# Attention values placed behind the next pair's scores, and their block sums multiplied in 64x32 tiles

## The chip, the core and the metric

The kernel runs on one core of a Trainium2 chip. The core has five engines that run side by side, each through its own instruction stream: TensorE (PE, matrix products out of SBUF into PSUM; its weight loads are shown apart as PEld), VectorE (DVE), ScalarE (ACT), GpSimd (POOL) and SyncE (SP, which here issues the transfers). [...] The metric is the device time of one execution in microseconds (us), lower is better.

## What is computed

Two blocks follow each other. The first is a sparse attention over 4 batches, 8 heads, 768 tokens and 64 numbers per head. Each token attends to the tokens less than 16 away, and to 24 sums, one for each block of 32 tokens (the maximum of the block's keys, the mean of its values):

```python
k_sum = k.reshape(B, H, nb, block, D).max(axis=3)
v_sum = v.reshape(B, H, nb, block, D).mean(axis=3)
scores_l = scale * (q @ k^T), outside |i - j| < 16 set to -1e9
scores_s = scale * (q @ k_sum^T) + log(block)
a = softmax over [scores_l, scores_s]
x = a @ concat([v, v_sum])
```

The second block takes x as (4, 768, 512), adds to it the real part of its two-dimensional Fourier transform (u), normalises each row, and applies two dense layers of 512 to 2048 to 512 with a ReLU between, added to u. All is in 32-bit floats.

## The kernel before

The dense layers are most of PE's work. For each batch they run in four phases: `gen_hidden(b, 0)`, `gen_out(b, 0)`, `gen_hidden(b, 1)`, `gen_out(b, 1)`, each over half of the 2048 inner columns. The products are of blocks two by two with seven multiplications; L1368 is the one of the hidden layer (128x128 weights, 384 columns), L1437 the one of the output layer (256 columns), L1414 batch 0's output. DVE and ACT add up the partial results from PSUM (L571, in the helper `tt`, and L1379 to L1398), and four PSUM buffers rotate among them, so a late DVE stops PE in the end.

Attention of batch b+1 is woven into the dense phases of batch b as a generator, `gen_attention`: `drive` advances both by so many steps (`yield`s), 80 of attention to 44 of the dense work for batches 2 and 3. Where in PE's stream the attention lands thus depends on the count of yields. Behind that a scheduler fixes the order of each engine's instructions when the program is built, by its own estimate of readiness; it can also cut a visit in pieces, with dense matmuls between them.

The heads go in four pairs (g = 0 to 3) for each batch. For one pair of batches 1 to 3 there are two visits to PE:

- *scores*: `scores` (L791, 48 matmuls in 64x64 tiles of the array: two heads, two halves of the tokens, blocks of 32 queries against 64 keys around them), then ACT's exponential of each half (L797) and DVE's multiplication by the mask `near` (L571); and `sum_scores` (L808, 4 matmuls in 64x32 tiles: queries against the block maxima) with its exponential (L809).
- *values*: `scale_sums` (L814: one matmul picks the pair's block sums of v into PSUM, and ACT writes them twice into `vs`, L816), then `values`: 48 matmuls in 64x32 tiles of 65 columns (L826, the probabilities of one block against its values and a column of ones), and 6 matmuls in 64x128 tiles of 130 columns (L831, the probabilities of the block sums against `vs`), into the same two PSUM tiles `av`. DVE takes the reciprocal of the sums (L836) and writes the scaled result into x (L571).

Every 32-bit matmul is two passes of the hardware, each with its weight load, so the profile's counts are twice those above. A tile of 64x32 uses a quarter of the array's columns and half of its rows: eight of them stand in the array at once.

The tag `attn` has four PSUM buffers, given out in the order of the code: `vs`, the two halves of the scores, the sum scores, the two `av`. The probabilities `p` have two buffers. Loads of values (`load_values`), of dense weights and of q and k stand in one queue on SP, in the order of issue. Batch 0 has another form (`wide_values`) that the change doesn't touch.

For batches 2 and 3 the last pair is followed by `turn_tiles`: two of x's token tiles go out to DRAM and come back with the tokens in mirrored order (L954 and L955, issued by POOL), and `fold_batch` then adds and subtracts halves of x for the Fourier transform, on DVE, with the returned tiles as `xr`. Between the two stand a number of yields.

Of the kernel before, what the change touches and what calls it, by code (L numbers as in the profile page):

```python
# [16 lines left out]
P = 128  # L17
# [471 lines left out]
def _main_program(ctx, tc, q, k, v, moe_w_ch1, moe_w_ch2, out):  # L489


    nc = tc.nc
# [6 lines left out]
    NP = H // 2  # L499
# [6 lines left out]
    HT = NST // 2  # L506
# [35 lines left out]
    vs = cpool.tile([P, 2, D1], FP, name="vs")  # L542
# [13 lines left out]
    def abank(shape, name):  # L556
        return psum.tile(shape, FP, tag="attn", bufs=4, name=name)
# [12 lines left out]
    def tt(out, in0, in1, op):  # L570
        return nc.vector.tensor_tensor(out=out, in0=in0, in1=in1, op=op).ins  # L571
# [28 lines left out]
    def room(name):  # L600
        return bpool.tile([P, NC * 2 * S], FP, tag="room", name=name)
# [62 lines left out]
    def load_values(b, g):  # L664
        if is_wide(b):
            load_wide_values(b, g)
            return
        load_narrow_values(b, g)

    def load_wide_values(b, g):  # L670

        vw, off = wide_vw(g), v[b, 2 * g].offset
        for r0, r1, i0, i1 in ((0, WK, 1, NQ - 1), (W, WK, 0, 1), (0, WK - W, NQ - 1, NQ)):
            for e in range(2):
                fetch(out=vw[r0:r1, e, i0:i1, 0:D],
                      in_=bass.AP(v.tensor, off + (S * e + QB * i0 - W + r0) * D,
                                  [[D, r1 - r0], [QB * D, i1 - i0], [1, D]]))

    def load_narrow_values(b, g):


        vw = vw_bufs[g % 2]
        if g < 2 and is_wide(b - 1):
            nc.gpsimd.memset(vw[:, :, D:D1], 1.0)
        for e in range(2):
            off = v[b, 2 * g + e].offset
            for h in range(2):
                r, i = 64 * (e ^ h), NB2 * h
                last = (b, g, e, h) == (B - 1, NP - 1, 1, 1)
                if last:  # L690

                    fetch(out=vw[r + 64 - W:r + 64, i:nb - 1, 0:D],
                                      in_=bass.AP(v.tensor, off + (BLOCK * i + 64 - 2 * W) * D,
                                                  [[D, W], [BLOCK * D, NB2 - 1], [1, D]]))
                n = 64 - W if last else 64
                fetch(out=vw[r:r + n, i:i + NB2, 0:D],
                                  in_=bass.AP(v.tensor, off + (BLOCK * i - W) * D, [[D, n], [BLOCK * D, NB2], [1, D]]))

    def key_maxima(g):
        nc.vector.tensor_reduce(out=km_bufs[g % 2][:, 0:nb], in_=kt_bufs[g % 2][:, W:W + S].rearrange("p (n f) -> p n f", f=BLOCK),  # L700
                                op=ALU.max, axis=AX.X)
# [100 lines left out]
    def sum_scores(b, g, p):  # L802
        km, qt = km_bufs[g % 2], nat[b, g]
        ps = abank([P, S2], f"ss_{b}_{g}")
        for h in range(2):
            for e in range(2):
                rows, r = slice(D * e, D * (e + 1)), 64 * (e ^ h) + 32 * h
                nc.tensor.matmul(ps[r:r + 32, :], km[rows, :], qt[rows, S2 * h:S2 * (h + 1)], start=True, stop=True)  # L808
        nc.scalar.activation(out=p, in_=ps, func=AF.Exp, scale=SC)  # L809

    def scale_sums(b, g):
        ps = abank([P, D], f"vs_{b}_{g}")
        vb, pick = sums[b, g]
        nc.tensor.matmul(ps, pick, vb, start=True, stop=True)  # L814
        for r in range(2):
            nc.scalar.activation(out=vs[:, r, 0:D], in_=ps, func=AF.Identity, scale=half_of[:, r:r + 1])  # L816

    def values(b, g, p, pm, x):
        vw = vw_bufs[g % 2]
        av = [abank([P, NST, D1], f"av_{b}_{g}_{r}") for r in range(2)]  # L820
        for t in range(NST):
            h = t // HT
            for j in range(4):
                for r in range(2):
                    rows, i = slice(64 * r, 64 * (r + 1)), 4 * t + j
                    nc.tensor.matmul(av[r][32 * j:32 * (j + 1), t, :], p[rows, h, i - NB2 * h, :], vw[rows, i, :],  # L826
                                     start=(t == 0), stop=False, skip_group_check=True)
        for t in range(HT):
            for r in range(2):
                rows = slice(64 * r, 64 * (r + 1))  # L830
                ins = nc.tensor.matmul(av[r][:, t:t + HT + 1:HT, :], pm[rows, P * t:P * (t + 1)], vs[rows],  # L831
                                       start=False, stop=(t == HT - 1), skip_group_check=True)
        marks["av", b, g] = ins.ins
        for r in range(2):
            rc = rec[:, b * NP + g, r]
            nc.vector.reciprocal(out=rc, in_=av[r][:, :, D])  # L836
            xo = x[:, 0, P * g + D * r:P * g + D * (r + 1)]
            xo = bass.AP(xo.tensor, xo.offset, [list(xo.ap[0]), [HT * DM + D * (1 - 2 * r), 2], [DM, HT], [1, D]])
            tt(xo, av[r].rearrange("p (h t) d -> p h t d", h=2)[:, :, :, 0:D],
               rc.rearrange("p (h t) -> p h t", h=2)[:, :, :, None].to_broadcast([P, 2, HT, D]), ALU.mult)  # L840
# [3 lines left out]
    def following(b, g, n):  # L844
        i = b * NP + g + n
        return divmod(i, NP) if i < B * NP else None
# [59 lines left out]
    def split_fold(b, fold):  # L906

        n = 3 * HT * DM
        zqs[b] = fold[:, n:n + 2 * HT * P].rearrange("p (r t m) -> p r t m", r=2, t=HT)
        return fold[:, 0:n].rearrange("p (i t d) -> p i t d", i=3, t=HT)  # L910
# [76 lines left out]
    def gen_attention(b):  # L987
        x = bpool.tile([P, NST, DM], FP, tag="x", bufs=2, name=f"x_{b}")
        x_of[b] = x
        held = None  # L990
        if b == 2:
            load(2, 1)
            load(2, 2)
        if b > 1:
            yield
            yield
            with tc.issue_after(marks["load"]):
                block_sums(b, 0)
            for _ in range(2):
                yield  # L1000
        for g in range(NP + 1):
            n1, n3 = (following(b, g, n) for n in (1, 3))
            if held:
                if b > 1:
                    scale_sums(b, g - 1)
                values(b, g - 1, *held, x)
                if n1 and b > 1:
                    load_values(*n1)
            if g == NP and b > 1:
                turn_tiles(b, x)  # L1010
                for _ in range(17):
                    yield
                rooms[b] = room(f"fold_{b}")
                steps = fold_batch(b, split_fold(b, rooms[b]))
                while True:
                    with tc.issue_after(marks["dense"]):
                        done = next(steps, steps) is steps
                    if done:
                        break
                    yield  # L1020
            elif held:
                for _ in range(5 if b > 1 else 1):
                    yield
            if g < NP:
                with tc.issue_after(marks["tile"]) if (b, g) == (1, 0) else ExitStack():
                    held = scores(b, g)
                if (b, g) == (1, 1):
                    with tc.issue_after(marks["mx", 0]):
                        key_maxima(g)
                sum_scores(b, g, held[1])  # L1030
            if g and n1 and b == 1:
                load_values(*n1)
            if g == 1 and b > 1:
                block_sums(b, 1)
            if g == NP and b > 1:
                return
            yield
            if g == NP:
                return
            for _ in range(2 if g == 0 and b > 1 else 0):  # L1040
                yield
            if (b, g) == (1, 0):
                for h in range(2):
                    with tc.issue_after(marks["un", 0]):
                        tt(held[0][:, h], held[0][:, h], near[:, h], ALU.mult)
            if n1:
                prepare(*n1, *((1,) if b > 1 else ()))
            if b == 1:
                scale_sums(b, g)
            if b > 1:  # L1050
                yield
                yield
                if n1:
                    prepare(*n1, 0)
            if n3 and not (b == 1 and n3 > (2, 0)):
                load(*n3)
            yield
            if b > 1:
                yield
# [561 lines left out]
```

## Time and profile before

| | |
|---|---|
| median of 3 runs | 794.84 us (793.83 to 795.17) |
| the profiled execution | 793.7 us |
| its span | 791.9 us |
| granted clock of TensorE | 0.999 |
| PE busy | 776.3 us, 98% |
| DVE busy | 492.0 us, 62% |
| ACT busy | 224.7 us, 28% |
| moved by DMA | 121.82 MB, 153 GB/s |

The span is the time from the profile's first instruction to its last; the execution's time is 1.8 us more. Times in the text below are us from the start of the span. In the list of costliest groups L1368 and L1437 lead; of the attention's lines on PE, L791 has 19.5 us, L826 15.9, L831 12.2 and L808 11.8 of modelled busy time, which overlaps since matmuls are pipelined. A line of the timeline joins equal instructions that stand together: start, length, engine, line, operation, names, tile of the array, shape and count.

### The profile page before, as it was taken

The numbers are of one execution on the slowest core, as the hardware profiler recorded it, in microseconds if no ns is written. First come the engines' busy times: TensorE is split into PE (matmuls) and PEld (weight loads), VectorE is DVE, ScalarE is ACT, GpSimd is POOL, SyncE is SP. The second block draws the span as 40 slices with busy tenths as digits, with TensorE's granted clock in tenths as the row PEclk, the third lists the DMA queues.
The fourth block names the chain that finished last, engine by engine and source line by source line (L and its number), as shares of the span: only waits on it lengthen the run. The fifth ranks groups of instructions, "written<-read, shape, count | busy, mean of one in ns | idle before, by whom it ended". The sixth has DMA issues, their size and how long they took to land.

```text
span 791.9 us, 14352 instructions
## 1 busy us (share of the span) xinstructions
PE 776.3 (98%) x5920; PEld 562.9 (71%) x5920; DVE 492.0 (62%) x1019; ACT 224.7 (28%) x491; POOL 47.9 (6%) x85
## 2 busy tenths in 40 slices
PE   8998999999999999999999999999999999999997
PEld 6777655445588866787578866788569875886686
DVE  5899988787988556752758544653677623533352
ACT  3564757226525022100236012200226111001200
POOL 0000000000000020200210020300120000000000
PEclk9999999999999999999999999999999999999999
DMA  9999787695956179976342169610614153106001
GB/s 212 189 262 246 190 268 190 210 284 201 240 186 152 46 206 263 218 110 184 137 153 94 54 208 211 183 55 11 243 37 140 54 215 134 51 0 233 0 28 56
DMA packets 133353, 121.82 MB, mean 154 GB/s; under 512 B 94464, under 2 KB 114912, under 8 KB 133088
## 3 DMA queue, kind: packets, MB, share of 16 engines
q1 hardware_dynamic: 132160, 118.53, 54.0%
q0 software_dynamic: 576, 2.10, 0.8%
q8 instruction: 48, 0.79, 0.4%
q10 hardware_dynamic: 544, 0.20, 0.1%
q14 instruction: 25, 0.20, 0.1%
HBM read 97.22 MB, written 23.59 MB: 153 GB/s over the span
## 4 chain that ended last, share of the span: by engine, by line
PE 88%; DVE 5%; ACT 4%; DMA 2%; issue 1%; DVEq 0%
PE hx L1368 19%; PE ox L1437 18%; PE hz L1368 9%; PE oz L1437 9%; PE hy L1368 5%; PE o L1414 5%; PE oy L1437 5%; PE y L1252 3%; PE sc L791 2%; PE mx L1211 2%; PE av L826 2%; PE unt L1342 1%; PE av L831 1%; DMA qn<-in_q_dram 1%; PE ss L808 1%; ACT kt L727 1%
## 5 line engine op out<-in xcount | busy, mean ns | idle before, releaser
L1368 PE MATMUL hx<-u,w 128*128 128x384 f32 x512 | 185.4, 491 | 2.4 <-ACT h L1385 1.0
L1368 PEld LDWEIGHTS hx<-u,w 128*128 128x128 f32 x512 | 95.2, 190 | 71.3 <-ACT p L797 3.8
L1368 PE MATMUL hz<-u,w 128*128 128x384 f32 x256 | 93.0, 486 | 0.0
L1437 PE MATMUL oz<-w,s 128*128 128x256 f32 x336 | 81.3, 380 | 0.0
L1437 PE MATMUL ox<-w,s 128*128 128x256 f32 x336 | 80.1, 380 | 0.0
L1437 PE MATMUL ox<-w,h 128*128 128x256 f32 x336 | 79.6, 381 | 0.0
L571 DVE TENSOR_TENSOR x<-ox,x 128x256 f32<-128x256 f32 x84 | 35.5, 422 | 66.2 <-PE ox L1437 65.9
L1368 PEld LDWEIGHTS hz<-u,w 128*128 128x128 f32 x256 | 48.6, 190 | 33.9
L1437 PEld LDWEIGHTS ox<-w,h 128*128 128x128 f32 x336 | 63.1, 190 | 10.8 <-issue 1.2
L1437 PEld LDWEIGHTS ox<-w,s 128*128 128x128 f32 x336 | 63.2, 190 | 9.1 <-DVE x L571 0.3
L1437 PEld LDWEIGHTS oz<-w,s 128*128 128x128 f32 x336 | 63.3, 190 | 8.9 <-DVE x L571 0.4
L1379 ACT COPY h<-hx 128x384 f32<-128x384 f32 x32 | 15.3, 477 | 191.6 <-PE hx L1368 191.5
L571 DVE TENSOR_TENSOR h<-hy,h 128x384 f32<-128x384 f32 x32 | 17.8, 557 | 48.9 <-PE hy L1368 48.8
L1368 PE MATMUL hy<-u,w 128*128 128x384 f32 x128 | 46.8, 487 | 0.0
L571 DVE TENSOR_TENSOR h<-hx,h 128x384 f32<-128x384 f32 x32 | 17.8, 556 | 45.2 <-PE hx L1368 44.0
L1414 PE MATMUL o<-w,h 128*128 128x512 f32 x96 | 42.2, 595 | 0.7 <-DVE w L571 0.7
L1398 ACT ACTIVATE h<-hx 128x384 f32<-128x384 f32 x32 | 15.7, 489 | 89.4 <-PE hx L1368 89.4
L1437 PE MATMUL oy<-w,h 128*128 128x256 f32 x168 | 40.1, 380 | 0.0
L571 DVE TENSOR_TENSOR x<-oz,x 128x256 f32<-128x256 f32 x42 | 17.8, 423 | 30.4 <-PE oz L1437 30.1
L1368 PEld LDWEIGHTS hy<-u,w 128*128 128x128 f32 x128 | 24.2, 190 | 17.1 <-DVE h L571 0.7
L1437 PEld LDWEIGHTS oy<-w,h 128*128 128x128 f32 x168 | 31.8, 190 | 4.4
L1414 PEld LDWEIGHTS o<-w,h 128*128 128x128 f32 x96 | 18.0, 190 | 23.6 <-issue 20.7
(166 smaller groups left out, 1072.5 us busy)
## 6 DMA issues: line engine op xcount, KB each, us to landing
w<-dw SPq DMA_DIRECT2D x44, 896.0 KB, 5.6
words<-in_moe_w_ch_dram SPq DMA_DIRECT2D x32, 512.0 KB, 5.8
dw<-w SPq DMA_DIRECT2D x12, 896.0 KB, 7.0
vw<-in_v_dram SPq DMA_DIRECT2D x47, 192.0 KB, 6.2
out_dram<-x SPq DMA_DIRECT2D x23, 256.0 KB, 2.0
vb<-in_v_dram SPq DMA_DIRECT2D x24, 192.0 KB, 7.2
kn<-in_k_dram SPq DMA_DIRECT2D x9, 384.0 KB, 6.3
qn<-in_q_dram SPq DMA_DIRECT2D x9, 384.0 KB, 6.9
```

What stands on the lines that cost most here:

```text
L571: return nc.vector.tensor_tensor(out=out, in0=in0, in1=in1, op=op).ins
L727: nc.scalar.copy(out=dst[D * e:D * (e + 1), s:S:2], in_=ps[D * s:D * (s + 1)])
L791: nc.tensor.matmul(ps[h][r:r + 64, i, :], kt[rows, o:o + 64], qt[rows, o:o + BLOCK], start=True, stop=True)
L808: nc.tensor.matmul(ps[r:r + 32, :], km[rows, :], qt[rows, S2 * h:S2 * (h + 1)], start=True, stop=True)
L826: nc.tensor.matmul(av[r][32 * j:32 * (j + 1), t, :], p[rows, h, i - NB2 * h, :], vw[rows, i, :], start=(t == 0), stop=False, skip_group_ch ...
L1211: nc.tensor.matmul(out, y[:, g], table, start=False, stop=True, skip_group_check=True)
L1252: nc.tensor.matmul(y, fgs[b][par][:, st, P * g:P * (g + 1)], fs[par][:, g % 2, st, :], start=(st == 0), stop=(st == n - 1))
L1368: ins = nc.tensor.matmul(ps, w[:, a, kk, :], u[:, r, kk, :], start=start and kk == 0, stop=stop and kk == 1, skip_group_check=True)
L1379: nc.scalar.copy(out=c11, in_=X)
L1398: nc.scalar.activation(out=c21, in_=X, func=AF.Relu)
L1414: nc.tensor.matmul(ps, h[:, n, hf, P * t:P * (t + 1)], wt[2, b, j][:, 2 * hf:2 * hf + 2, :], start=(n, hf) == (0, 0), stop=(n, hf) == (NC ...
L1437: nc.tensor.matmul(ps, left[a][:, n, :], wt[2, b, j][:, r, :], start=start and n == 0, stop=stop and n == NC - 1, skip_group_check=True)
```

## The change

Two things are changed.

In `values`, the six matmuls of L831 become 24: each 128-column tile is written as four of 32 columns, so that they use the same 64x32 tiles as L826. The loop takes the four column tiles in turn and the two row halves inside.

In `gen_attention`, the values of pair g−1 are, for some g, no longer a visit of their own but stand directly behind the scores and sum scores of pair g. Such a step is `joined`: g = 1, 2, 3 of batches 2 and 3, and g = 3 of batch 1. There `scale_sums` of pair g−1 comes ahead of the scores, and the load of the values' next buffer behind the joined visit. The last pair's values stay alone. For batches 2 and 3 eight yields are put ahead of them, and nine in place of 17 follow `turn_tiles`, so that the number of steps stays.

```diff
--- before.py
+++ after.py
@@ -826,10 +826,11 @@
                     nc.tensor.matmul(av[r][32 * j:32 * (j + 1), t, :], p[rows, h, i - NB2 * h, :], vw[rows, i, :],
                                      start=(t == 0), stop=False, skip_group_check=True)
         for t in range(HT):
-            for r in range(2):
-                rows = slice(64 * r, 64 * (r + 1))
-                ins = nc.tensor.matmul(av[r][:, t:t + HT + 1:HT, :], pm[rows, P * t:P * (t + 1)], vs[rows],
-                                       start=False, stop=(t == HT - 1), skip_group_check=True)
+            for j in range(4):
+                for r in range(2):
+                    rows, o = slice(64 * r, 64 * (r + 1)), 32 * j
+                    ins = nc.tensor.matmul(av[r][o:o + 32, t:t + HT + 1:HT, :], pm[rows, P * t + o:P * t + o + 32], vs[rows],
+                                           start=False, stop=(t == HT - 1), skip_group_check=True)
         marks["av", b, g] = ins.ins
         for r in range(2):
             rc = rec[:, b * NP + g, r]
@@ -1000,7 +1001,11 @@
                 yield
         for g in range(NP + 1):
             n1, n3 = (following(b, g, n) for n in (1, 3))
-            if held:
+            joined = (1 if b > 1 else 3) <= g < NP
+            if b > 1 and g == NP:
+                for _ in range(8):
+                    yield
+            if held and not joined:
                 if b > 1:
                     scale_sums(b, g - 1)
                 values(b, g - 1, *held, x)
@@ -1008,7 +1013,7 @@
                     load_values(*n1)
             if g == NP and b > 1:
                 turn_tiles(b, x)
-                for _ in range(17):
+                for _ in range(9):
                     yield
                 rooms[b] = room(f"fold_{b}")
                 steps = fold_batch(b, split_fold(b, rooms[b]))
@@ -1022,12 +1027,19 @@
                 for _ in range(5 if b > 1 else 1):
                     yield
             if g < NP:
+                past = held
+                if joined and b > 1:
+                    scale_sums(b, g - 1)
                 with tc.issue_after(marks["tile"]) if (b, g) == (1, 0) else ExitStack():
                     held = scores(b, g)
                 if (b, g) == (1, 1):
                     with tc.issue_after(marks["mx", 0]):
                         key_maxima(g)
                 sum_scores(b, g, held[1])
+                if joined:
+                    values(b, g - 1, *past, x)
+                    if n1 and b > 1:
+                        load_values(*n1)
             if g and n1 and b == 1:
                 load_values(*n1)
             if g == 1 and b > 1:
```

## The prediction

> **What bounds the kernel now.** I first read the page's busy row and its chain of waits, to find the engine whose time counts. TensorE (PE) is busy 98% and carries 88% of the chain, at full granted clock (0.999).
>
> ```profile
> PE 776.3 (98%) x5920; PEld 562.9 (71%) x5920; DVE 492.0 (62%) x1019; ACT 224.7 (28%) x491; POOL 47.9 (6%) x85
> PE 88%; DVE 5%; ACT 4%; DMA 2%; issue 1%; DVEq 0%
> ```
>
> Since an average can hide stages, I next read the table of busy time by stretches (start:end, length, PE, PEld, DVE, ACT, POOL busy, clock, DMA share, GB/s). Batch 1's attention lies mostly in the first stretch shown, batch 2's in the second, batch 3's in the third.
>
> ```profile
> 66.00:160.00 94.00, 89.33 (x884) 51.82 (x883) 80.40 (x146) 52.60 (x91) 0.00 (x0) 1.00 0.80 218
> 282.00:372.00 90.00, 89.72 (x1124) 66.01 (x1123) 52.26 (x102) 13.83 (x35) 14.47 (x16) 1.00 0.83 185
> 460.00:545.00 85.00, 84.48 (x1102) 60.60 (x1101) 44.34 (x89) 14.78 (x36) 13.68 (x16) 1.00 0.59 153
> ```
>
> In batches 2 and 3 PE idles for 0.3 and 0.5 us of 90 and 85, and DVE has some 40 us free: a nanosecond off PE's stream there is a nanosecond off the end. Batch 1's stretch is different: DVE 80 of 94, PE idle 4.7 us; what is saved in it may be waited away.
>
> Third, PE's timeline around one values visit (L814, L826, L831) and one scores visit (L791, L808) of batch 2, with dense matmuls (L1368) between. Busy times overlap, so only the starts are subtracted.
>
> ```profile
> 310.64 1.45 PE L1368 MATMUL hx<-u,w 128*128 128x384 f32 x4
> 311.93 0.33 PE L814 MATMUL vs<-vbs,sel 96*128 96x64 f32 x2
> 312.19 1.20 PE L826 MATMUL av<-vw,p 64*32 64x65 f32 x96
> 313.32 0.94 PE L831 MATMUL av<-vs,p 64*128 64x130 f32 x12
> 314.19 1.56 PE L1368 MATMUL hx<-u,w 128*128 128x384 f32 x4
> 315.59 1.45 PE L1368 MATMUL hy<-u,w 128*128 128x384 f32 x4
> 318.17 1.45 PE L1368 MATMUL hz<-u,w 128*128 128x384 f32 x4
> 319.55 1.60 PE L791 MATMUL sc<-qt,kt 64*64 64x32 f32 x96
> 321.08 0.85 PE L808 MATMUL ss<-qt,km 64*32 64x384 f32 x8
> 321.86 1.56 PE L1368 MATMUL hx<-u,w 128*128 128x384 f32 x4
> ```
>
> A dense group of four costs 1.29 (310.64 to 311.93), the first group after a visit 1.40 (314.19 to 315.59). A values visit costs 314.19 − 311.93 + 0.11 = 2.37 us. A scores visit: it starts 0.09 late (319.55 against 318.17 + 1.29), lasts 2.31, and has the 0.11 behind it: 2.51. The 0.09 and 0.11 recur wherever the tile shape changes: in single instructions 0.09 passes between the last column streamed and the next weight load, and 0.107 is that load with nothing to cover it.
>
> **The change, part by part.**
>
> *Block sums in 64x32 tiles (12 visits, 24 matmuls for 6 in each).* L831's twelve passes stream from 313.43 to 314.10, 0.67 us. Before that lie 0.09 and 0.107, because L826 has 64x32 tiles and L831 64x128. After, both have one shape, and 0.20 goes. The streaming: 48 passes of 130 columns over eight tiles are six rounds. A round of eight 65-column passes in L826 took 54 ns at first (weight loads 6.7 ns apart) and 67 later, so six rounds of twice the columns take 0.65 to 0.80; I take 0.67, as six passes of 0.1115 now. Net −0.20 a visit (bounds −0.22 and −0.07). The evacuation by DVE and L826 are untouched.
>
> [...]
>
> *Values behind the next scores (7 visits: pairs 1 to 3 of batches 2 and 3, and batch 1's third pair behind its fourth).* Now 2.37 + 2.51 = 4.88. After, from the same starts: L814 0.26, L791 1.53, L808 0.69 (0.78 less 0.09: L826 has the same shape), L826 1.04 (1.13 less 0.09), block sums 0.67 + 0.09, then 0.11: 4.39, and some of L826's first weight loads now lie under L808. I take 4.36, so −0.52 a visit with the new tiles; × 7 = −3.6. Batch 1's has no L814 in it and saves the same.
>
> *Values that stay alone (5).* Batch 1's first pair waits three times (0.6, 0.3 and 0.6 us idle at 76.0, 77.0 and 78.7, for ACT): its 0.2 is mostly waited away, −0.1. Batch 1's second and fourth and batch 3's last: −0.2 each, −0.6. Batch 2's last is next.
>
> *Where the scheduler cuts visits.* The order of PE's instructions is fixed when the program is built, and differs beyond the diff. Batch 2's last values are cut in three now:
>
> ```profile
> 353.88 0.33 PE L814 MATMUL vs<-vbs,sel 96*128 96x64 f32 x2
> 354.14 0.54 PE L826 MATMUL av<-vw,p 64*32 64x65 f32 x24
> 354.62 2.86 PE L1437 MATMUL ox<-w,h 128*128 128x256 f32 x12
> 357.41 0.88 PE L826 MATMUL av<-vw,p 64*32 64x65 f32 x48
> 358.22 0.93 PE L831 MATMUL av<-vs,p 64*128 64x130 f32 x6
> 359.08 1.13 PE L1437 MATMUL ox<-w,h 128*128 128x256 f32 x4
> 360.14 0.54 PE L826 MATMUL av<-vw,p 64*32 64x65 f32 x24
> 360.62 0.93 PE L831 MATMUL av<-vs,p 64*128 64x130 f32 x6
> 361.48 1.78 PE L1437 MATMUL oy<-w,h 128*128 128x256 f32 x7
> ```
>
> From 353.88 to 361.48 are 7.60; the 16 dense passes inside cost 0.215 each (eight from 352.16 to 353.88), 3.44; with the 0.11 the visit costs 4.27. In the changed order it is whole, 2.17: −2.1. Batch 1's third sum scores, cut now (2 passes at 103.52 after 0.57 idle for ACT, 6 at 116.18), become whole: at least a change of shape, 0.3; at most also wait and pass time, 1.4; −0.3 by the near end, as DVE is nearly full there. Two cuts are new: batch 1's last values after two matmuls, and batch 3's last scores after three. A cut costs 0.09 + 0.2 + 0.11, +0.4 each: +0.8.
>
> *New waits.* The tag of attention's PSUM has four buffers. In a joined visit they go to the sums of values, two score halves, sum scores, and then to the two halves of values: the first waits for ACT's reading of the sums (over 2 us old), the second for ACT's exponential of score half 0. That ran from 321.19 to 321.68 while L808 streamed until 321.77, so it is 0.1 ahead. Behind it, in PE's order, stands the rest of the visit. If ACT is one conversion late (batch 1) it costs up to 1 us once. DVE: after the visit two masks (2.76 us from 321.71) and the evacuation (1.3 us at 314.30) now come together, ahead of an addition that PE's buffers need; PE already idles 0.28 there at 325. Bounds 0 and 0.4 a visit; I take 0.1 for both waits: +0.7.
>
> *Moved beside.* The values' loads are issued one step later on SP's queue, behind weight loads of 896 KB (2.2 us each); they are used a full pair later, so nothing. The last pair's exchange through DRAM starts later: x's tiles 2 and 5 go out and come back reordered (POOL's two DMAs). In batch 2 it ran from 362.7 to 373.9 and DVE first used it at 384.30; in batch 3, undisturbed, it took 523.6 to 531.3 for a use at 565.74. In the changed order the last values stand some 2 us ahead of the end of the first output phase, 371.94 and 553.38, which the use follows by 12.4. So the exchange starts at about 372 and 553, takes 7.7, and of a cover of 10.4 and 34 us some 4.5 is left, 0 if both of its transfers wait for one 896 KB load (2.2 us each). I take 0 here, with up to 4 us in batch 3, where four weight loads (9 us) are issued at the same moment.
>
> [...]
>
> **Sum.** −3.6 −0.1 −0.6 −2.1 −0.3 +0.8 +0.7 = −5.2. The profiled execution took 793.7 (span 791.9 and 1.8 around it), so 788.5; the median shown, 794.84, lies 1.1 above it, so 789.6.
>
> **Rivals.**
> 1. *The tiles do not stream side by side at 130 columns* (slower). The four column tiles share rows and a PSUM bank. If pairs of them took turns, the block sums would take 1.34 and each visit lose 0.67 × 12 = 8.0: 797.6; all in turn, 2.7 us, 814. It decides from 0.43 a visit on. Against it: in L826 the same eight tiles, into the same two banks, run 96 passes of 54 ns in 1.04 us, five at a time.
> 2. *The tiles give nothing*: rounds at the slow pace of L826, 0.80. +0.13 × 12 = 1.6: 791.2.
> 3. *A wait takes the gain.* The exchange returns late in batch 3 (+2 to 4), and DVE's tail costs the full 0.4 (+2.1 over the 0.1 taken): 792 to 796, about no change. For it: all four loads stand ahead at one moment. Against it: DVE's 40 free us.
> 4. *More is saved*: no waits, and the cut in batch 1 gives 1.4: 787.5.
>
> **How the numbers follow.** Two tenths of a per cent, 1.6 us, is about what a measurement of this kernel can tell from no change. Chances: forecast and rival 4 together 0.62, rival 2 0.13, rival 3 0.16 (half of it still faster, half the same), rival 1 0.09 (slower, a fifth of it only the same). With what I overlook: faster 0.80, same 0.10, slower 0.10. The range 786.5 to 795.0 takes in rivals 2 to 4, leaving out rival 1.
>
> **What would show it.** The block sums' weight loads at 32 columns, 48 passes in 0.65 to 0.8 us, without 0.2 us ahead; joined visits of 4.3 to 4.4 us from first L814 to 0.11 behind the last pass; batch 2's last values whole; PE busy near 771. I am wrong if the new passes stand over 20 ns apart, if the second half of L826 shows idle time for ACT, or if DVE's addition of the reordered tiles waits for a DMA and PE idles after it.

## The result and the profile after

The changed kernel took 806.5 us (median of 5; 805.29 to 807.6) against 794.84 (median of 5 in the same comparison; 793.33 to 795.81): ratio 1.014, interval 1.0125 to 1.0155. It is slower by 1.4%, where 0.7% faster was forecast. The profiled execution took 805.29 us, its span 803.4, and the mean granted clock was 0.993.

The page's busy row and chain of waits, which answer to the first fence of the prediction:

```profile
PE 776.2 (97%) x6352; PEld 564.3 (70%) x6352; DVE 489.9 (61%) x1019; ACT 224.8 (28%) x491; POOL 47.2 (6%) x85
PE 84%; DVE 8%; ACT 4%; DMA 2%; issue 2%; SPq 0%; DVEq 0%
```

PE is as busy as before (776.2 against 776.3 us) in a span 11.5 us longer. In those 11.5 us it stood still, or part of its work ran slower.

The three stretches of the prediction's table again, with the same columns:

```profile
66.00:160.00 94.00, 88.23 (x850) 50.02 (x850) 79.34 (x139) 52.65 (x91) 0.00 (x0) 1.00 0.78 218
282.00:372.00 90.00, 85.48 (x1187) 63.55 (x1187) 49.38 (x98) 14.09 (x35) 11.88 (x14) 0.98 0.77 160
460.00:545.00 85.00, 81.72 (x1102) 59.59 (x1101) 42.69 (x82) 14.43 (x34) 11.56 (x14) 1.00 0.56 141
```

In batch 2's stretch PE idles 4.5 us where it idled 0.3, in batch 3's 3.3 where it idled 0.5. The list of PE's waits (total, times, longest) names the largest:

```profile
PE av L832 <- issue: 6.0, 3, 2.7
PE hx L1380 <- DVE h L571: 3.5, 1, 3.5
PE av L826 <- issue: 2.4, 3, 0.9
```

There are 8.4 us under "issue", for which the profile shows no releaser, and one wait of 3.5 us for DVE. Of the 8.4, 0.6 stand in batch 1's first values visit and are in the kernel before too (76.03); the other 7.8 are the five stalls that follow. (The line numbers have moved with the edit: L832 is the block sums, L1380 the hidden layer, L1449 the output layer. In the experiments they move again by some lines.)

**The stalls without a releaser.** PE's timeline at the joined visit of batch 2's third pair:

```profile
317.80 0.33 PE L814 MATMUL vs<-vbs,sel 96*128 96x64 f32 x2
318.06 1.60 PE L791 MATMUL sc<-qt,kt 64*64 64x32 f32 x96
319.59 0.85 PE L808 MATMUL ss<-qt,km 64*32 64x384 f32 x8
320.24 1.14 PE L826 MATMUL av<-vw,p 64*32 64x65 f32 x92
...
321.24 0.66 PE L832 MATMUL av<-vs,p 64*32 64x130 f32 x26
324.63 0.63 PE L832 MATMUL av<-vs,p 64*32 64x130 f32 x19 [2.74 <-issue]
325.19 2.29 PE L1380 MATMUL hx<-u,w 128*128 128x384 f32 x3
```

PE stops for 2.7 us in the middle of the loop of block sums, between two matmuls of which the second waits for nothing new. The transfers of that gap, 321.7 to 324.6 (queue, packets, MB, share of the 16 DMA engines):

```profile
q1 hardware_dynamic: 1598, 0.93, 107.1%
q8 instruction: 1, 0.02, 2.0%
```

One packet of the instruction queue fell into the gap. In the trace it moves 16,384 bytes from 322.30 to 323.25, and PE goes on 1.38 us later. Of the five stalls in the joined visits of batches 2 and 3, every one ends so. Counting all of PE's records from 0 at the start of the trace (weight loads, matmuls and semaphore waits), PE goes on each time with a record of the same number modulo 256. "Stops" is the last start ahead of the stall, "goes on" the first start behind it:

```
visit (batch, pair of the scores)  PE stops and goes on   record  modulo 256  packet landed  goes on after
2, second                          303.44 to 304.52       5569    193         303.16         1.36
2, third                           321.62 to 324.63       6337    193         323.25         1.38
2, fourth                          346.11 to 347.24       6849    193         345.69         1.55
3, second                          490.67 to 493.22       9153    193         491.85         1.38
3, third                           508.88 to 510.14       9665    193         508.77         1.37
```

So the reading is: PE's own instructions arrive in pieces of 256, and in the joined visits PE uses them up faster than the next piece comes. A matmul of this kernel is four instructions in that stream (two passes, each with its weight load: the 48 matmuls of L826 are 96 passes in the trace of before, and the page above counts 6352 of either kind). A values visit had 220 of them before and a scores visit 208; a joined visit has 500, in 4.3 us.

**The wait for DVE.** In batch 3 the exchange through DRAM came back too late. DVE's and PE's timelines there:

```profile
570.08 0.56 DVE L571 TENSOR_TENSOR h<-hy,h 128x384 f32<-128x384 f32 x1 [1.98 <-PE hy L1380]
574.92 0.69 DVE L571 TENSOR_TENSOR fold<-xr 128x512 f32<-128x512 f32 x1 [4.28 <-DMA xr<-turned,mirror]
```

```profile
573.68 1.45 PE L1380 MATMUL hz<-u,w 128*128 128x384 f32 x4
578.61 5.49 PE L1380 MATMUL hx<-u,w 128*128 128x384 f32 x8 [3.47 <-DVE h L571]
583.89 1.83 PE L1380 MATMUL hy<-u,w 128*128 128x384 f32 x4
```

DVE stands 4.28 us at the addition that reads the returned tiles, and PE 3.47 us behind it. POOL's timeline has the two transfers of the exchange, and the issues from 558 to 570 (median us from issue to landing at the end) show what ran beside them: two of the four weight loads issued from 557.10 to 558.49, and a fifth at 567.42.

```profile
558.01 0.75 POOL L955 DMA_DIRECT2D turned<-x  x1 [52.80 <-DVE ok L1586]
569.50 1.03 POOL L956 DMA_INDIRECT xr<-turned,mirror  x1 [10.74 <-ACT h L1391]
```

```profile
w<-dw SPq DMA_DIRECT2D x3, 896.0 KB, 11.2
turned<-x POOLq DMA_DIRECT2D x1, 512.0 KB, 10.7
xr<-turned,mirror POOLq DMA_INDIRECT x1, 5.4
```

**The clock.** The eight passes from 578.61 to 583.89, behind the wait for DVE, took 5.28 us, where eight take 2.58 elsewhere (565.94 to 568.52): the granted clock was 0.50 there. It fell behind the 2.7 us stall too, as these stretches show (the granted clock is the third value from the end):

```profile
324.60:326.00 1.40, 1.37 (x21) 0.86 (x22) 0.81 (x4) 0.00 (x0) 1.29 (x2) 0.72 0.66 99
326.00:327.00 1.00, 1.00 (x3) 0.67 (x2) 0.44 (x1) 0.00 (x0) 0.88 (x2) 0.50 0.49 79
327.00:328.00 1.00, 1.00 (x3) 0.42 (x2) 0.00 (x0) 0.00 (x0) 0.86 (x3) 0.50 0.24 35
328.00:329.00 1.00, 1.00 (x4) 0.56 (x3) 0.81 (x2) 0.00 (x0) 0.53 (x2) 0.69 1.01 166
329.00:330.00 1.00, 1.00 (x5) 0.60 (x4) 0.34 (x2) 0.00 (x0) 0.00 (x0) 1.00 0.96 156
```

What the clock lacks in these rows adds up to 1.7 us, or 3.4 us at half clock. PE counted as busy all the while, which is why its busy time didn't fall with the work.

**Where the time went.** The same dense matmul in both traces gives the difference at that point: the start of batch 1's hidden layer +0.16 us, its second hidden phase +3.01, the start of batch 2's +3.02, its second hidden phase +4.82, the start of batch 3's +11.53, the last output matmul +11.53.

```
stretch                       difference  stalls in visits  exchange  half clock                what is left
batch 2's attention           +2.85       5.2               -         1.7 (0.66 over 5 us)      -4.1
batch 3's attention           +1.80       3.8               -         -                         -2.0
exchange of batch 3's x       +6.71       -                 3.5       3.0 (0.50, 0.90 of 5 us)  +0.2
```

(The stalls are counted from start to start in the table of stalls, so each holds the usual step of up to 0.1 us. The clock's price is its lack times the stretch: 0.34 × 5; 0.50 × 5 and 0.10 × 5.) What the change saves is there, 6.1 us in the last column's first two rows, and 17.2 us of new stops and slow clock lie on top.

### The profile page after: what moved, and what is told of

Same layout as the page of the kernel before. It is cut to its first block, busy times and chain, and to the rows that moved or that the text cites. A ratio compares the mean times of both kernels' runs of the same rounds, so it can differ in the third digit from the quotient of the medians.

```text
span 803.4 us, 15208 instructions
## 1 busy us (share of the span) xinstructions
PE 776.2 (97%) x6352; PEld 564.3 (70%) x6352; DVE 489.9 (61%) x1019; ACT 224.8 (28%) x491; POOL 47.2 (6%) x85
## 4 chain that ended last, share of the span: by engine, by line
PE 84%; DVE 8%; ACT 4%; DMA 2%; issue 2%; SPq 0%; DVEq 0%
PE hx L1380 19%; PE ox L1449 18%; PE oz L1449 9%; PE hz L1380 9%; PE hy L1380 5%; PE oy L1449 5%; PE o L1426 4%; PE y L1264 3%; PE mx L1223 2%; PE sc L791 2%; PE unt L1354 1%; PE av L826 1%; PE ss L808 1%; PE av L832 1%; DVE w L571 1%
## 5 line engine op out<-in xcount | busy, mean ns | idle before, releaser
L1380 PE MATMUL hx<-u,w 128*128 128x384 f32 x512 | 188.9, 499 | 5.7 <-DVE h L571 3.5
L1380 PEld LDWEIGHTS hx<-u,w 128*128 128x128 f32 x512 | 96.9, 193 | 74.9 <-DVE h L571 5.7
L1380 PE MATMUL hz<-u,w 128*128 128x384 f32 x256 | 93.7, 488 | 0.0
L1449 PE MATMUL oz<-w,s 128*128 128x256 f32 x336 | 81.1, 380 | 0.0
L1449 PE MATMUL ox<-w,s 128*128 128x256 f32 x336 | 80.0, 379 | 0.0
L1449 PE MATMUL ox<-w,h 128*128 128x256 f32 x336 | 79.1, 380 | 0.0
L1380 PEld LDWEIGHTS hz<-u,w 128*128 128x128 f32 x256 | 48.9, 191 | 34.7 <-issue 0.9
L1449 PEld LDWEIGHTS ox<-w,h 128*128 128x128 f32 x336 | 63.2, 190 | 10.1 <-issue 0.8
L1449 PEld LDWEIGHTS oz<-w,s 128*128 128x128 f32 x336 | 63.4, 190 | 8.8 <-DVE x L571 0.4
L1449 PEld LDWEIGHTS ox<-w,s 128*128 128x128 f32 x336 | 63.4, 190 | 8.6 <-DVE s L571 0.3
L1380 PE MATMUL hy<-u,w 128*128 128x384 f32 x128 | 47.2, 490 | 1.4 <-DVE h L571 1.4
L1449 PE MATMUL oy<-w,h 128*128 128x256 f32 x168 | 40.0, 379 | 0.0
L1380 PEld LDWEIGHTS hy<-u,w 128*128 128x128 f32 x128 | 24.5, 193 | 18.4 <-DVE h L571 1.5
L1449 PEld LDWEIGHTS oy<-w,h 128*128 128x128 f32 x168 | 31.9, 190 | 4.3
```

The costliest lines, as they stand in the source:

```text
L1380: ins = nc.tensor.matmul(ps, w[:, a, kk, :], u[:, r, kk, :], start=start and kk == 0, stop=stop and kk == 1, skip_group_check=True)
L1449: nc.tensor.matmul(ps, left[a][:, n, :], wt[2, b, j][:, r, :], start=start and n == 0, stop=stop and n == NC - 1, skip_group_check=True)
```

## The experiments

Two theories, stated before the runs. F: the instruction stream runs dry, because a visit uses up a piece of 256 instructions in less time than the next takes to come. W: joining brings waits for data or buffers (PSUM of `attn`, ACT's exponential, DVE), and "issue" only hides which. Both hold the exchange for the cause of the 3.5 us. The kernel before was measured beside the kernels of each comparison; its medians were 796.16 us beside the first four, 795.95 beside the others, so ratios count.

### The tiles alone

```diff
 kernel before
-            for r in range(2):
-                ... av[r][:, t:t + HT + 1:HT, :], pm[rows, P * t:P * (t + 1)], vs[rows] ...
+            for j in range(4):
+                for r in range(2):
+                    ... av[r][o:o + 32, t:t + HT + 1:HT, :], pm[rows, P * t + o:P * t + o + 32], vs[rows] ...
```

> The kernel before with the block sums in 64x32 tiles and nothing else; no visit is joined. A values visit then issues 292 PE instructions (four for each matmul) in place of 220. Theory F (the instruction stream runs dry: it comes in pieces of 256 instructions, and a piece that is used up in less than about 4 us is followed by a stall): a whole piece fits into a values visit only when its border falls in the first 36 instructions, so at most two short stalls; 12 visits x 0.20 saved; 792 to 796 us. Theory W (the stalls of the changed kernel are waits for data or buffers that joining brings): no stall at all, 792.4 us. If instead the tiles do not stream side by side, above 798 us.

Measured: 797.64 us, ratio 1.0015 (0.9995 to 1.0036), no gain that can be told from none, and outside the expected 792 to 796. The tiles do what they should: the first values visit of batch 3 lasts from 482.87 to 484.97, 2.10 us, where it lasted 2.26 (477.97 to 480.23).

```profile
482.87 0.33 PE L814 MATMUL vs<-vbs,sel 96*128 96x64 f32 x2
483.13 1.14 PE L826 MATMUL av<-vw,p 64*32 64x65 f32 x92
...
484.12 0.91 PE L832 MATMUL av<-vs,p 64*32 64x130 f32 x45
484.97 1.24 PE L1369 MATMUL hx<-u,w 128*128 128x384 f32 x3
```

That is 0.16 a visit, 1.9 for twelve. Two stalls that the kernel before doesn't have stand in the profile at records 193 modulo 256: 1.04 us in batch 1's second scores (84.60 to 85.64) and 0.96 two dense matmuls behind a values visit (303.37 to 304.33), each 1.4 to 1.5 us after a packet landed. They take 2.0 us, as much as the tiles save. The second shows that the visit need not hold the stall: 292 instructions in a row are enough to meet it behind the visit.

### The joining alone

```diff
 changed kernel
-            for j in range(4):
-                for r in range(2):
-                    ... (64x32 tiles)
+            for r in range(2):
+                ... (64x128 tiles, as before)
```

> The changed kernel with the block sums in 64x128 tiles as before: the visits are joined but issue 428 PE instructions in place of 500. Theory F: the stalls stay in two to five of the seven joined visits, at another place of the visit than in the changed kernel, since the borders of 256 fall elsewhere; with the late exchange of batch 3 and the clock that drops behind each long stall 799 to 806 us. Theory W: the stalls stay where they were, behind the same instructions of the same five visits.

Measured: 806.43 us, ratio 1.0132 (1.0089 to 1.0175), just above the 799 to 806 that F expected, and in the profile 7.1 us of "issue" in L826 and L831, 0.6 of them the wait that the kernel before has as well. Three of the seven joined visits stall: batch 1's (165.26 to 168.78), batch 2's third pair (326.16 to 328.93), batch 3's third (512.26 to 513.14), again at records 193 modulo 256. Behind the first two the clock stood at 0.50 over the next 5 us. Batch 1's visit didn't stall in the changed kernel and does here, with the same buffers and producers. W had expected the same five visits. The yields of the changed kernel are in this run, so it is the joining together with them that it prices.

### The exchange early

```diff
 changed kernel
             if b > 1 and g == NP:
-                for _ in range(8):
+                for _ in range(0):
                     yield
...
-                for _ in range(9):
+                for _ in range(17):
                     yield
```

> The changed kernel with the yields of the last pair put back as they were (none ahead of the values, 17 behind the exchange). Both theories: DVE no longer waits 4.3 us for the tiles that come back in batch 3, PE no longer idles 3.5 us at 575 and the half clock behind it is gone, together -4.5 to -6: 800.5 to 802 us, with the stalls inside the joined visits as before. If the exchange is not the cause, 806 us.

Measured: 803.3 us, ratio 1.009 (1.0059 to 1.0122), in place of 1.014: some 4 us less, where 4.5 to 6 were expected. Batch 3's exchange is issued at 547.36 in place of 558.01, ahead of the weight loads; no wait for it is left, and between batch 2's second hidden phase and the start of batch 3's nothing is lost against the kernel before. Four stalls stay in the joined visits (1.8, 1.2, 3.1 and 1.5 us), at the same instructions as in the changed kernel; the fifth, in batch 2's second pair, is gone: its packet moved 0.7 us before PE began the piece ahead of it (302.53 against 303.22) and not 0.75 after. The old yields also have a price: batch 2's last values are cut in three again. From 357.88 to 366.43 they take 3.8 us without the 22 dense passes between (0.216 each), where the changed kernel's whole visit takes 2.1 (371.02 to 373.12). That hides 1.7 us of what the early exchange saves. So the exchange is the cause of its 3.5 us and of the half clock behind it, and the smaller part of the loss.

### The same instructions, shifted by half a piece

```diff
 changed kernel, at the start of the program
     for i in range(2):
         nc.tensor.matmul(ps, zeros[:, 512:640], zeros[:, 0:512], start=True, stop=True)
+    for i in range(32):
+        nc.tensor.matmul(ps[:, 0:16], zeros[:, 512:640], zeros[:, 0:16], start=True, stop=True)
```

> The changed kernel with 32 matmuls of 16 columns more at the very start, while PE waits for its first loads: 128 PE instructions that cost no time, and nothing else moves. Theory F: the borders of the pieces fall half a piece elsewhere, so every stall inside a joined visit stands 128 PE instructions earlier or later in its visit, its number in the stream still 193 modulo 256, each 0.8 to 3 us; the total anywhere within 4 us of 806. Theory W: the stalls stand at the same instructions of the same five visits and have the same lengths (1.0, 2.9, 1.1, 2.4, 1.2 us).

Measured, in one execution: 823.62 us, far outside the expected 4 us around 806. My "cost no time" was wrong: the 64 passes ran from 4.93 to 15.48, with the clock at 0.57 from 10 to 20, and put what follows over 10 us later (15.48 against 5.11 for the next matmul). What the run was for came out sharply. Instructions from the start of the joined visit to its stall:

```
visit         changed kernel   shifted   difference
2, second     268              396       +128
2, third      462              334       -128
2, fourth     337              465       +128
3, second     486              358       -128
3, third      425              297       -128
```

All stay at records 193 modulo 256. The third pair of batch 2, which stopped at the block sums, now stops in L826:

```profile
338.14 1.60 PE L791 MATMUL sc<-qt,kt 64*64 64x32 f32 x96
339.68 0.85 PE L808 MATMUL ss<-qt,km 64*32 64x384 f32 x8
340.32 0.83 PE L826 MATMUL av<-vw,p 64*32 64x65 f32 x61
343.76 0.52 PE L826 MATMUL av<-vw,p 64*32 64x65 f32 x34 [2.61 <-issue]
```

Batch 1's joined visit, which had no stall, has one of 4.7 us here, and batch 3's fourth pair one of 0.7; both lie outside the expected 0.8 to 3. No wait for data moves with the count of instructions ahead of it; W falls.

The other traces say the same. In the ten traces of this document PE sits idle for over 0.4 us under "issue" 44 times. Ten of these are the wait of 0.64 us in batch 1's first values visit, one in each trace. The other 34 all end at a record 193 modulo 256, 1.0 to 1.6 us after a packet of the instruction queue landed.

### Local values issued twice, nothing joined

```diff
 kernel before, values()
+        for _ in range(2):
-        for t in range(NST):
+            for t in range(NST):
                 ... (the 48 matmuls of L826)
```

> The kernel before with the 48 matmuls of the local values issued twice in every visit of batches 1 to 3 (the second pass starts the sums anew): 412 PE instructions a visit, no visit joined, no new buffer and no new wait. Theory F: in four to eight of the 12 values visits a stall of 0.5 to 3 us without a named releaser, each at an instruction whose number in the stream is 193 modulo 256; with 1.0 us of work more a visit and some half-clock stretches 811 to 822 us. Theory W: no stall, 794.8 + 12 = 807 us.

Measured, in one execution: 831.06 us, 9 above F's upper end. Six of the twelve values visits stall at records 193 modulo 256, by 1.9 to 5.6 us, and one scores visit by 0.75. The list of waits and the longest stall (L827 is the loop that is issued twice, L832 the block sums in their old tiles):

```profile
PE av L827 <- issue: 12.8, 5, 4.7
PE av L832 <- issue: 6.9, 2, 5.3
```

```profile
329.60 0.72 PE L832 MATMUL av<-vs,p 64*128 64x130 f32 x8
335.60 0.80 PE L832 MATMUL av<-vs,p 64*128 64x130 f32 x4 [5.29 <-issue]
```

Here no visit is joined, so many instructions alone bring the stalls. I had undersized them. In the longest, PE stops at 330.04, and the packet moves only from 333.09 to 334.19, 3 us into the stall. What held it back isn't settled by these runs.

### Batch 2's last visit whole

```diff
 kernel before
+            if b == 2 and g == NP:
+                for _ in range(4):
+                    yield
             if held:
...
-                for _ in range(17):
+                for _ in range(13 if b == 2 else 17):
                     yield
```

> The kernel before, nothing joined and no new tiles, with four yields ahead of batch 2's last values and four fewer behind them: in the order of the built program that visit is then whole in place of three pieces, and batch 3 is untouched. The prediction's price of the cuts: -2.1, so 0.997 of the kernel before. A values visit has 220 instructions, so theory F sees no stall. If the cuts cost less than thought, between 0 and -1.

Measured: 794.38 us, ratio 0.9972 (0.9955 to 0.9988): 0.28%, some 2.2 us, faster than the kernel before, and so than both. The visit that was in three pieces:

```profile
362.26 0.33 PE L814 MATMUL vs<-vbs,sel 96*128 96x64 f32 x2
362.52 1.20 PE L826 MATMUL av<-vw,p 64*32 64x65 f32 x96
363.65 0.94 PE L831 MATMUL av<-vs,p 64*128 64x130 f32 x12
364.52 2.00 PE L1440 MATMUL ox<-w,s 128*128 128x256 f32 x8
```

In the traces the visit takes 2.37 us (364.52 − 362.26 + 0.11) in place of 4.27, 1.9 less; the other 0.2 of the prediction's 2.1 are the tiles, which this kernel doesn't have. This step of the prediction held, and it has nothing to do with joining or tiles.

### The whole visit, and the tiles in batch 3

```diff
 kernel of the last experiment, in values()
-            for r in range(2):
-                rows = slice(64 * r, 64 * (r + 1))
-                ins = ... (64x128 tiles)
+            for j in range(4 if b == 3 else 1):
+                for r in range(2):
+                    ... (64x32 tiles in batch 3, 64x128 else)
```

> The kernel of the whole last visit of batch 2, and the block sums in 64x32 tiles in batch 3 alone (292 instructions in its four values visits). By theory F a visit of 292 can hold a whole piece only if a border falls into its first 36 instructions: most likely none or one stall of 1 us, and four times 0.2 saved: 0 to -0.8 against the whole visit alone, 0.996 to 0.998 of the kernel before.

Measured: ratio 1.0011 (0.9991 to 1.0032), not the expected 0.996 to 0.998: the whole visit's gain is gone. The profiled execution, at 794.39 us, was one of the faster of its twelve and explains this only in part: the first two visits of batch 3 last 2.10 us each, but PE stops twice for 0.3 us, at 517.28 and 521.44, where three visits follow within 10 us, with few dense matmuls between. Both stops are at records 193 modulo 256. The scheduler also cuts batch 3's last values: 30 of the 48 passes of the block sums stand alone at 539.51, 18 us behind the others, a cut that the prediction prices at 0.4. The rest of the loss isn't settled.

### The late exchange alone

```diff
 kernel before
+            if b > 1 and g == NP:
+                for _ in range(8):
+                    yield
             if held:
...
-                for _ in range(17):
+                for _ in range(9):
                     yield
```

> The kernel before with the changed kernel's yields alone (eight ahead of the last values and nine behind the exchange, batches 2 and 3), nothing joined and no new tiles. Both theories: batch 2's last values whole (-2.1), and in batch 3 the exchange comes back behind the four weight loads, DVE waits some 4 us for it, PE idles 3.5 us, and up to 3 us more go in the half clock behind that: +1.5 to +4.5, 0.2 to 0.6% slower than the kernel before. If the exchange is hidden without the joined visits: -2.

Measured: 794.53 us, ratio 0.9977 (0.9964 to 0.9991). What both theories expected didn't come; the other branch, -2, did. Batch 2's last visit is whole, but batch 3's exchange isn't late: it is issued at 524.5 us, as in the kernel before (523.6), since the scheduler keeps batch 3's last values at 520.56 in spite of the eight yields. The programs run some us apart, so I count back from the start of batch 2's second hidden phase:

```
kernel                                             exchange issued   us ahead of the phase
before                                             523.65            29.7
the late exchange alone (yields alone)             524.52            29.7
the tiles alone                                    545.73            12.2
the exchange early (joined, tiles, old yields)     547.36            12.3
the joining alone (joined, new yields, old tiles)  562.42            0.2
changed                                            558.01            0.2
```

The tiles move the exchange by 17 us without any joining: the scheduler then puts the last 30 passes of batch 3's last values at 543.43. Of these six, DVE waits for the exchange only where it is issued 0.2 us ahead. The yields alone don't bring the wait, nor do the joining and the tiles with the old yields. No run has the joining with both the old yields and the old tiles.

## Why the prediction was wrong

**The step that failed** is a term the sum doesn't have, the supply of PE's instructions, put at nothing without a reason. The prediction counted 36 more passes a values visit and weighed them against the array (streaming, tile shape), and it costed joining by waits on buffers, ACT and DVE. It never asked whether PE's instructions themselves arrive in time. Stalls for them took 9.0 us from start to start (7.8 as idle time in the profile) and the half clock behind one of them 1.7, against a forecast gain of 5.2. The shifted stream and the doubled values show this cause; undoing either half of the change shows that the joining with its yields carries most of it (ratio 1.0132), while the tiles lose to stalls about as much as they save (1.0015).

The trace of before had the sign of it. PE's timeline of batch 0, a stretch that no edit touches and no step of the prediction uses:

```profile
26.70 0.38 PE L748 MATMUL sc<-qt,kt 64*96 64x64 f32 x3
27.58 1.07 PE L748 MATMUL sc<-qt,kt 64*96 64x64 f32 x21 [0.51 <-issue]
```

This stop in the middle of one loop ends at PE's record 705, which is 193 modulo 256, and 1.35 us after an instruction packet landed at 26.24.

**The exchange** was in the text, and taken at 0 with "up to 4 us in batch 3". It took 3.5 us of PE's time, and 3.0 of half clock that no step had. Its start and its use were forecast well, at 553 and 565.74: the changed kernel, 4.8 us later by then, has 558.01 and 570.64. What was mis-sized is its length beside the weight loads, 7.7 us forecast and 16.9 measured (558.01 to 574.92). The outgoing transfer alone took 10.7, where it took 3.2 in the kernel before, so the 0 taken for it didn't hold. The 7.7 was also read too short: in the kernel before the second transfer lands at 532.09 and not 531.3, so 8.4 us. Rival 3 had the place and the mechanism and sized it at 2 to 4; with the clock it was 6.5.

**Terms that held.** The joined visit: 4.36 us forecast; in batch 2's second pair it took 300.76 to 306.09, less 1.08 of stall, plus the 0.11 behind it, 4.36. The block sums: −0.20 forecast, −0.16 measured. Batch 2's last visit whole: −2.1 forecast with the tiles; −1.9 in the trace without them, −2.2 by the run, whose interval is 1.0 to 3.6 us. The waits on buffers and engines were small: ACT's exponential held L826's weight loads up 1.1 us in six visits, 0.18 each, where 0.1 was taken for ACT and DVE together. What is left of batches 2 and 3 without stalls and clock, −4.1 and −2.0, is somewhat more than forecast (−3.4 and −1.1: three joined visits at −0.52 each, three times +0.1 of waits, batch 2's whole visit or batch 3's cut and its last values).

**Batch 1** gave nothing: the start of batch 1's hidden layer stands at +0.16 us, though the program was 0.69 ahead at 70 us, ahead of any edit. The prediction had some 0.5 for its joined visit and more for the others, with the warning that DVE is near its limit there. In the stretch from 66 to 160 PE idles 5.8 us where it idled 4.7 (94.00 less 88.23 and 89.33), the longest for DVE, 1.38 at 103.62. No run separates the parts.

**Rival 1**, tiles that take turns, is refuted: with the tiles alone L826 and the block sums take 1.84 us to the next dense matmul (483.13 to 484.97), where they took 2.00 (478.23 to 480.23). The result lies on the rival's side for a reason that no rival named. (Rival 4's time adds up to 787.8 by its own terms, 0.7 and 1.1 below 789.6, and not 787.5.)

## What to carry to other kernels

Count the instructions that a change puts in a row on PE, and in how many microseconds they are used up. In these traces 256 instructions, 64 small matmuls, are one piece of the stream (the stalls end at records 193 modulo 256), and in the changed kernel's stalls the next piece could run 3.4 to 5.0 us after PE had begun the one before. The joined visits, 500 instructions in 4.3 us, stalled in five of seven cases, and in all seven when shifted. None of the values visits of 220, between dense matmuls, stalled in the kernel before.

A gap under "issue" between two matmuls of one loop can be a sign of this (of the 44 gaps under "issue" over 0.4 us in these traces, 34 were); compare its end with the instruction queue's packets. And a stop of PE can cost more than its own length: in the changed kernel the half clock behind the stops of 2.7 and 3.5 us took another 1.7 and 3.0 us.

## What the runs showed of the hardware

- The packets of the instruction queue q8 have 16,384 bytes (48 of them in the kernel before, 52 in the changed one), and the borders at which PE stalls lie 256 records apart. In the five stalls of the changed kernel the packet began 0.75 to 2.7 us after PE had begun the piece before (for the stall at 303.44: record 5313 at 301.07, packet at 301.82), took 0.9 to 1.35, and PE went on 1.36 to 1.55 after it. It had begun 2.3 to 2.7 us before PE went on; in the same trace, between dense matmuls and without a stall, the last packet ahead of a border began 4.3 us before PE's border record (478.14, the border at 482.44).
- In these five stalls the packet that PE waited for thus moved only after PE had begun the piece before it: that piece, 256 instructions, was the last that PE had at hand. The longest idle time at a border in these traces was 5.3 us (the doubled values).
- The clock halves behind some stops and not behind others: after 2.7 us at 321.7 and after 3.5 at 575 in the changed kernel it fell to 0.50; after 2.5 us at 490.7 in the same run, and after 3.1 at 491.3 in the kernel with the early exchange, it stayed at 1.00. Nothing here tells which it will be.
